# Order on VectorE's queue at the end of a half: the addition of two accumulators, the turning of the next pair, and dispatch steps

## The chip, the cores and the metric

The kernel runs on one core of one Trainium2 chip. The metric is the device time of one execution in microseconds (us). Three timed executions of the kernel before took 711.72, 712.66 and 712.91 us; their median, 712.66 us, is the time that the change is measured against. The profile shows one further execution, of 712.75 us, with a span of 711.0 us from the first to the last instruction of the program.

## The reference

Two stages in a row. The first is attention with a block mask (`_attn_ref`), on 4 batches of 8 heads, 768 positions and a head size of 64, all float32:

```
scores = scale * np.matmul(q, k.transpose(0, 1, 3, 2))
scores = np.where(mask, scores, -1000000000.0)
attn = np.exp(scores - max) / (sum + 1e-09)
x = np.matmul(attn, v)
```

The mask keeps blocks of 32 x 32: the diagonal and its neighbours, the first and last block row and column, and three sampled blocks per block row. The second stage (`_moe_ref`) takes the 3072 rows of 512 numbers, finds for each row the nearest of 8 experts by cosine similarity (largest logit), and passes the row through that expert alone: a matrix product with w1 (512 x 1024), a maximum with 0, a matrix product with w2 (1024 x 512), and a multiplication by the gate, the largest softmax probability.

## The kernel before

**Attention** (`attention_fast`, from L928). The work is cut into 192 units. A unit `u` belongs to a pair of heads (`g`, 12 units each, 16 pairs), to one half of the queries (`qh`, 384 of 768) and to one block of 128 keys (`kc`, 0 to 5). Six units make up a *half*: 384 queries of two heads against all keys. There are 32 halves.

For each unit, `score_fast` (L348) puts the mask and the scores into a PSUM tile `sc` by 12 groups of small matmuls (L358) and lets ScalarE take the exponential into a tile `e` (L361; four buffers, in the pool `ep`). `attend_fast` (L365) multiplies the values with `e` on TensorE and gathers the products of a half in PSUM, in the tile `av` (L379). The pool `acc` that holds `av` has one buffer, of two banks: one sum over the even and one over the odd 64 keys of each block. On VectorE the tiles `e` of a half are added up into `esum`, which gives the denominators later: the first addition of a half is L374 (`kc == 1`), the other four are L376. At the end of a half ScalarE copies one of the two accumulators into `part` (L383), and VectorE adds the other to it, giving `at` (L385). That addition is the last reader of `av`, so the first value matmul of the next half waits for it.

`settle` (L389), three units into the next half, turns `at` and `esum` back on TensorE (L407, L414) and divides on VectorE (L417 to L427). `squares` (L431) then takes the sum of squares of those rows on GpSimd (L438, L442).

**The next pair** is loaded by `load_blocks` (L254, its DMAs in L264, on SyncE's queue SP except for some of the first) and `load_pair` (L250), and turned by `turn_blocks` (L267): VectorE transposes its blocks of 32 x 32, first those of k (`kt<-kld`), and one unit later those of q (`qt<-qld`), two instructions each (L274). The raw tiles `kld` and `qld` have one buffer each, so the load of the pair after next follows the turn.

**Routing and dispatch** (`route` L491, `rank` L550, `dispatch_early` L655) are generators. After every batch, `after_sequence` (L910) makes a plan by hand: at which unit of the next batch which step is taken. The steps of `dispatch_early` come in the units 1, 2 and 4 of a half, from unit 22 on in the third batch and up to unit 8 in the fourth. The last batch is routed in `last_rows` (L1077), amid the first expert tile.

**Expert tiles** (`expert_tile` L835, `mixed_tile` L873). Rows are gathered by expert in tiles of 128, the matrix products run on TensorE, and the weights, 4 MB for each tile, come in by DMA (L807).

**Order.** The framework puts the instructions of each engine into one queue when the program is built. It keeps to the order of the source among what its model takes to be ready, but it may move one instruction ahead of another. `issue_after(x)` forbids that for one case: each instruction made inside the block which runs on the same engine as `x` stands behind `x` in that engine's queue. It adds no semaphore. In `attention_fast` the planned steps stand behind `n.summed`, `n.exps` and `n.tick` (L980: VectorE, ScalarE, SyncE), and `turn_blocks` behind `n.summed` (L988). In the kernel before, `n.summed` is always the newest addition into `esum` (L374 or L376), never `at`.

Of the kernel before, what the change touches and what calls it, by code (L numbers as in the profile page):

```python
# [15 lines left out]
ALU = mybir.AluOpType  # L16
# [8 lines left out]
NC = S // P  # L25
# [21 lines left out]
HALF = S // 2  # L47
# [317 lines left out]
def attend_fast(k, u):  # L365
    nc = k.nc
    g, qh, kc = u // (2 * NC), u // NC % 2, u % NC
    e, v = k.es[u], k.loaded[g][2]
    if kc == 0:
        k.av = k.acc.tile([P, 2, 512], F32, name="av", tag="av")  # L370
        k.first = e
    elif kc == 1:
        k.esum = k.sp.tile([P, 2, HALF], F32, name="esum", tag="esum")
        k.summed = nc.vector.tensor_tensor(out=k.esum, in0=k.first, in1=e, op=ALU.add)  # L374
    else:
        k.summed = nc.vector.tensor_tensor(out=k.esum, in0=k.esum, in1=e, op=ALU.add)  # L376
    for r in range(2):
        for h in range(2):
            nc.tensor.matmul(k.av[D * h:D * (h + 1), r, 0:HALF], lhsT=v[D * r:D * (r + 1), h, kc, :],  # L379
                             rhs=e[D * r:D * (r + 1), h, :], start=(kc == 0), stop=(kc == NC - 1))  # L380
    if kc == NC - 1:
        part = k.sp.tile([P, HALF], F32, name="part", tag="part")
        nc.scalar.copy(out=part, in_=k.av[:, 1, 0:HALF])  # L383
        at = k.sp.tile([P, HALF], F32, name="at", tag="at")
        nc.vector.tensor_tensor(out=at, in0=k.av[:, 0, 0:HALF], in1=part, op=ALU.add)  # L385
        k.done[u // NC] = (at, k.esum)


# [85 lines left out]
def logits(k, x):  # L474
    nc, p = k.nc, k.rp
    lg = two_banks(k, "lg")[:, 0, 0:NC * E].rearrange("p (c e) -> p c e", e=E)
    for c2 in range(0, NC, 2):
        ps = k.big.tile([P, 2 * ND, P], F32, name="xt_ps", tag="big")
        for i in range(2 * ND):
            c, d = c2 + i // ND, i % ND  # L480
            nc.tensor.transpose(ps[:, i, :], x[:, c, d * P:(d + 1) * P], k.ident)
        xt = p.tile([P, 2 * ND, P], F32, name="xt")
        nc.vector.tensor_copy(out=xt, in_=ps)
        for c in (c2, c2 + 1):
            for d in range(ND):
                nc.tensor.matmul(lg[:, c, :], lhsT=xt[:, (c - c2) * ND + d, :], rhs=k.en[:, d, :],
                                 start=(d == 0), stop=(d == ND - 1))
    return lg


def route(k, b):  # L491

    nc, p, x = k.nc, k.rp, k.x[b]
    nrm = p.tile([P, NC], F32, name="nrm")
    if k.exact:
        for c in range(NC):
            sq = p.tile([P, DM], F32, name="sq")
            nc.scalar.activation(sq, x[:, c, 0:DM], ACT.Square, accum_out=nrm[:, c:c + 1])
    else:
        nsq = k.nsq[b]  # L500
        nc.gpsimd.tensor_tensor(out=nsq[:, :, 0:2], in0=nsq[:, :, 0:2], in1=nsq[:, :, 2:4], op=ALU.add)
        nc.gpsimd.tensor_tensor(out=nrm.unsqueeze(2), in0=nsq[:, :, 0:1], in1=nsq[:, :, 1:2], op=ALU.add)
    nc.gpsimd.tensor_tensor(out=nrm, in0=nrm, in1=k.half, op=ALU.pow)

    def wide(t):
        return t.unsqueeze(2).broadcast_to([P, NC, E])

    l = p.tile([P, NC, E], F32, name="l")
    lg = logits(k, x) if k.exact else l
    if not k.exact:  # L510
        part = k.part[b]
        for w in (4, 2):
            nc.gpsimd.tensor_tensor(out=part[:, :, 0:w], in0=part[:, :, 0:w], in1=part[:, :, w:2 * w], op=ALU.add)
        nc.gpsimd.tensor_tensor(out=l, in0=part[:, :, 0], in1=part[:, :, 1], op=ALU.add)
    yield
    nc.vector.tensor_scalar(out=nrm, in0=nrm, scalar1=1e-6, scalar2=None, op0=ALU.add)
    nc.vector.reciprocal(out=nrm, in_=nrm)
    m = p.tile([P, NC], F32, name="mx")
    nc.vector.tensor_tensor(out=l, in0=lg, in1=wide(nrm), op=ALU.mult)
    nc.vector.reduce_max(out=m, in_=l, axis=AX.X)  # L520
    nc.vector.tensor_tensor(out=l, in0=l, in1=wide(m), op=ALU.subtract)
    yield
    ex = p.tile([P, NC, E], F32, name="ex_l")
    nc.scalar.activation(ex, l, ACT.Exp)
    oh = k.oh[:, b * NC:(b + 1) * NC, :]
    pick = p.tile([P, NC, E], F32, name="pick")
    nc.vector.tensor_scalar(out=pick, in0=l, scalar1=0.0, scalar2=None, op0=ALU.is_equal)
    nc.vector.tensor_tensor(out=pick, in0=pick, in1=k.rev.unsqueeze(1).broadcast_to([P, NC, E]), op=ALU.mult)
    nc.vector.reduce_max(out=m, in_=pick, axis=AX.X)
    nc.vector.tensor_tensor(out=oh, in0=pick, in1=wide(m), op=ALU.is_equal)  # L530
    yield
    for c in range(NC):
        t = b * NC + c
        nc.gpsimd.tensor_tensor(out=k.seen[:, t + 1, :], in0=k.seen[:, t, :], in1=k.oh[:, t, :], op=ALU.add)
    for w in (4, 2):
        nc.gpsimd.tensor_tensor(out=ex[:, :, 0:w], in0=ex[:, :, 0:w], in1=ex[:, :, w:2 * w], op=ALU.add)
    gate = x[:, :, DM:XW]
    nc.gpsimd.tensor_tensor(out=gate, in0=ex[:, :, 0:1], in1=ex[:, :, 1:2], op=ALU.add)
    nc.gpsimd.tensor_scalar(out=gate, in0=gate, scalar1=1e-9, scalar2=None, op0=ALU.add)
    yield  # L540
    nc.vector.reciprocal(out=gate, in_=gate)
    yield
    drams = (k.x_early, k.x_dram) if b < EARLY else (k.x_dram,)
    for dram in drams:
        for c in range(NC):
            nc.sync.dma_start(out=dram[b * S:(b + 1) * S, :].rearrange("(c p) w -> p c w", c=NC)[:, c], in_=x[:, c])
            yield
# [362 lines left out]
def after_sequence(n, b):  # L910

    routing = partial(next, route(n, b), None)
    plan = [(7, routing), (14, routing), (16, routing), (17, routing), (20, partial(rank, n, b)), (23, routing)]
    plan += [(27 + NC * (i // 4), routing) for i in range(NC * (1 + (b < EARLY)))]
    if b == EARLY - 1:
        n.dispatching = partial(next, dispatch_early(n), None)
        plan += [(u, n.dispatching) for u in range(22, 45) if u % NC in (1, 2, 4)]
    if b == EARLY:
        plan += [(u, n.dispatching) for u in (1, 2, 4, 8)]
        plan += [(9, partial(fetch_rows, n, 0)), (10, partial(fetch_rows, n, 1))]  # L920
        for i, when in enumerate(((3, 3, 3, 9, 9, 9, 15, 15), (15, 21, 21, 21, 33, 33, 39, 39))):
            step = partial(next, fetch_weights(n, i, i, 4), None)
            plan += [(u, step) for u in when]
        plan += [(44, partial(prepare, n, 0))]
    return plan


def attention_fast(n, ctx):  # L928
# [34 lines left out]
    for u in range(units):  # L963
# [14 lines left out]
        for when, what in plan:  # L978
            if when == u % (per * NPAIR):
                with n.tc.issue_after(n.summed.ins), n.tc.issue_after(n.exps.ins), n.tc.issue_after(n.tick.ins):  # L980
                    what()

        steps = [partial(attend_fast, n, u)] + ([partial(score_fast, n, u + 2)] if u + 2 < units else [])
        for step in reversed(steps) if u % NC == 0 else steps:
            step()
# [12 lines left out]
def attention_exact(n, ctx):  # L998
# [14 lines left out]
    for u in range(units + 2):  # L1013
        if u < units:
            if u % per == 0 and u // per + 2 < pairs:
                load_pair(n, u // per + 2)
            score(n, u)
            if u % per == per - 3 and u // per + 1 < pairs:
                turn_pair(n, u // per + 1)
        if 1 <= u <= units:  # L1020
            turn_probs(n, u - 1)
        if u >= 2:
            attend(n, u - 2)
            if (u - 1) % (H * NC) == 0:
                b = (u - 1) // (H * NC) - 1
                for _ in route(n, b):
                    pass
                rank(n, b)
                if b == EARLY - 1:
                    for _ in dispatch_early(n):  # L1030
                        pass
# [145 lines left out]
```

## Time and profile before

| | |
|---|---|
| median of three runs | 712.66 us |
| profiled execution, its span | 712.75 us, 711.0 us |
| busy, share of the span: TensorE | 98% |
| VectorE, ScalarE, GpSimd | 47%, 27%, 32% |
| `sc` matmuls, q and k (L358) | 1536, 157.9 us |
| `av` matmuls (L379) | 1536, 154.9 us |
| `hp` matmuls of the experts (L845) | 1472, 169.1 us |
| `yp` matmuls (L858) | 368, 162.0 us |
| additions into `esum` (L374, L376) | 160, 162.3 us |
| additions `at` (L385) | 32, 0.55 us each |

How it is read: a row of the page's groups has the line, the engine, the operation, what it writes and reads, and the count; then busy us and ns of one; then the idle time of the engine just before these instructions, and who ended most of it. A row of the timeline has the start in us, the us that it covers, and the instruction; square brackets hold the idle time before it and its releaser. A row of the windows has the stretch, its length, and for each engine its busy us with the number of instructions.

Attention fills roughly the first 331 us; the expert tiles take the rest. PE is TensorE's matmuls, PEld its weight loads, DVE VectorE, ACT ScalarE, POOL GpSimd, SP SyncE.

### The profile page before, as it was taken

The page shows a single profiled execution, that of the slowest core. Times are in us where ns is not written, and L with a number is a line of the kernel's source. Part 1 is how long each engine was busy: PE and PEld are TensorE (multiplying, and loading weights), DVE is VectorE, ACT ScalarE, POOL GpSimd, SP SyncE. Part 2 cuts the span into 40 slices and gives each one's busy share as a digit, 9 for nine tenths or more (in the row PEclk, how much of TensorE's full clock was granted, in tenths as well). Part 3 has the DMA queues.
Part 4 walks back from the last instruction along what each step waited for, and adds up shares of the span by engine and source line. Part 5 has one row for each costly group of instructions (what it writes and reads, how often), then busy time and mean ns, then how long its engine had stood idle before and what let it go on. Part 6 is the DMA issues. An engine that isn't in the chain of part 4 may idle for free.

```text
span 711.0 us, 19426 instructions
## 1 busy us (share of the span) xinstructions
PE 693.6 (98%) x8313; PEld 436.5 (61%) x8313; DVE 332.6 (47%) x684; ACT 188.5 (27%) x266; POOL 230.0 (32%) x383
## 2 busy tenths in 40 slices
PE   9999999999999999999999999999999999999992
PEld 4555555555555554557767777676676756667771
DVE  6887778777878888765661111111111111111110
ACT  5455545555555455453000000000000000000000
POOL 1255466544764367545401111112111111112010
PEclk9999999999999999999999999999999999999997
DMA  7632333575326768553999989988899998999990
GB/s 133 116 63 43 59 68 69 128 135 122 65 41 155 127 157 219 193 165 113 274 398 397 368 319 344 337 321 302 313 405 397 400 333 313 404 396 396 343 320 18
DMA packets 180808, 164.76 MB, mean 232 GB/s; under 512 B 128284, under 2 KB 128284, under 8 KB 180710
## 3 DMA queue, kind: packets, MB, share of 16 engines
q1 hardware_dynamic: 174950, 149.80, 67.1%
q0 software_dynamic: 4160, 13.39, 4.8%
q8 instruction: 69, 1.13, 0.7%
q10 hardware_dynamic: 1600, 0.20, 0.2%
q14 instruction: 29, 0.24, 0.1%
HBM read 147.62 MB, written 16.01 MB: 230 GB/s over the span
## 4 chain that ended last, share of the span: by engine, by line
PE 90%; issue 3%; DVE 3%; POOL 1%; ACT 1%; DMA 1%; POOLq 0%; DVEq 0%; SPq 0%; ACTq 0%
PE hp L845 21%; PE yp L858 21%; PE sc L358 20%; PE av L379 17%; PE back L414 3%; PE hp L886 2%; PE yp L906 2%; PE xg_ps L830 1%; PE back L407 1%; ACT e L361 1%; PE warm L80 1%; DVE kt L274 1%; DVE esum L376 1%; DVE at L385 0%; DMA out_dram<-y,slot_l 0%
## 5 line engine op out<-in xcount | busy, mean ns | idle before, releaser
L361 ACT ACTIVATE e<-sc 128x768 f32<-128x768 f32 x192 | 155.7, 811 | 154.9 <-PE sc L358 149.7
L845 PEld LDWEIGHTS hp<-xgt,w 128*128 128x128 f32 x1472 | 167.7, 192 | 10.8 <-issue 10.2
L845 PE MATMUL hp<-xgt,w 128*128 128x128 f32 x1472 | 169.1, 275 | 0.0
L858 PE MATMUL yp<-w,h 128*128 128x512 f32 x368 | 162.0, 593 | 0.1
L358 PE MATMUL sc<-qt,kt 64*64 64x384 f32 x1536 | 157.9, 482 | 0.0
L379 PE MATMUL av<-e,vld 64*64 64x384 f32 x1536 | 154.9, 487 | 3.0 <-DVE at L385 2.8
L376 DVE TENSOR_TENSOR esum<-esum,e 128x768 f32<-128x768 f32 x128 | 131.6, 1028 | 40.4 <-ACT e L361 38.6
L858 PEld LDWEIGHTS yp<-w,h 128*128 128x128 f32 x368 | 68.0, 190 | 77.5 <-issue 76.3
L442 POOL TENSOR_TENSOR sq<-sq 128x192 f32<-128x192 f32 (+1 forms) x186 | 106.0, 570 | 13.9
L867 POOL DMA_INDIRECT out_dram<-y,slot_l x20 | 20.2, 1008 | 246.0 <-DVE y L866 233.9
L848 ACT ACTIVATE h<-hp 128x512 f32<-128x512 f32 x23 | 13.7, 597 | 298.3 <-PE hp L845 298.3
L379 PEld LDWEIGHTS av<-e,vld 64*64 64x64 f32 x1536 | 53.8, 133 | 61.0 <-issue 28.2
L866 DVE TENSOR_SCALAR y<-yp,xg 128x512 f32<-128x512 f32 x25 | 18.8, 751 | 140.7 <-PE yp L858 128.2
L358 PEld LDWEIGHTS sc<-qt,kt 64*64 64x64 f32 x1536 | 58.9, 133 | 38.5 <-issue 36.2
L852 DVE TENSOR_SCALAR h<-hp 128x512 f32<-128x512 f32 x23 | 15.9, 692 | 131.6 <-PE hp L845 131.6
L438 POOL TENSOR_TENSOR sq<-x 128x384 f32<-128x384 f32 x31 | 27.1, 874 | 121.9 <-DVE part L427 101.9
L358 PE MATMUL sc<-qmask,kmask 64*64 64x384 bf16 x768 | 65.9, 323 | 0.1
L358 PEld LDWEIGHTS <-kmask 64*64 64x64 bf16 x768 | 24.7, 107 | 33.1 <-issue 33.0
L374 DVE TENSOR_TENSOR esum<-e 128x768 f32<-128x768 f32 x32 | 30.7, 959 | 10.0 <-ACT e L361 9.4
L414 PE MATMUL back<-ones,esum 64*64 64x1 f32 x1536 | 26.4, 190 | 0.0
L414 PEld LDWEIGHTS back<-ones,esum 64*64 64x64 f32 x1536 | 25.6, 135 | 0.0
L785 POOL DMA_INDIRECT xg<-x_dram,slot_l x22 | 22.6, 1027 | 6.7 <-issue 6.7
(191 smaller groups left out, 361.4 us busy)
## 6 DMA issues: line engine op xcount, KB each, us to landing
w<-in_moe_w_dram SPq DMA_DIRECT2D x54, 2048.0 KB
w<-in_moe_w_dram SPq DMA_DIRECT2D x16, 512.0 KB
x_dram<-x SPq DMA_DIRECT2D x24, 256.5 KB
vld<-in_v_dram SPq DMA_DIRECT2D x32, 192.0 KB
kld<-in_k_dram SPq DMA_DIRECT2D x60, 96.0 KB
qld<-in_q_dram SPq DMA_DIRECT2D x60, 96.0 KB
x_early<-x SPq DMA_DIRECT2D x12, 256.5 KB
ticks<-dens SPq DMA_DIRECT2D x32, 0.0 KB
```

The lines of the kernel that those rows point to most:

```text
L358: nc.tensor.matmul(ps[D * r:D * (r + 1), h, 0:HALF], lhsT=rows[D * h:D * (h + 1), keys], rhs=cols[D * h:D * (h + 1), queries], start=first ...
L361: k.exps = nc.scalar.activation(e, ps[:, :, 0:HALF], ACT.Exp, scale=SCALE)
L374: k.summed = nc.vector.tensor_tensor(out=k.esum, in0=k.first, in1=e, op=ALU.add)
L376: k.summed = nc.vector.tensor_tensor(out=k.esum, in0=k.esum, in1=e, op=ALU.add)
L379: nc.tensor.matmul(k.av[D * h:D * (h + 1), r, 0:HALF], lhsT=v[D * r:D * (r + 1), h, kc, :], rhs=e[D * r:D * (r + 1), h, :], start=(kc == 0 ...
L414: nc.tensor.matmul(sums[D * s:D * (s + 1), t, h, r:r + 1], lhsT=esum[D * r:D * (r + 1), h, cols], rhs=k.ones[D * r:D * (r + 1), 0:1], star ...
L438: nc.gpsimd.tensor_tensor(out=sq, in0=x, in1=x, op=ALU.mult)
L442: k.squared = nc.gpsimd.tensor_tensor(out=out, in0=sq[:, :, 0:width], in1=sq[:, :, width:2 * width], op=ALU.add).ins
L785: k.nc.gpsimd.indirect_dma_start(out=x[:, :], out_offset=None, in_=(k.x_dram if late else k.x_early)[:, :], in_offset=bass.IndirectOffsetO ...
L845: nc.tensor.matmul(hp[:, f, :], lhsT=w1[:, d, (f0 + f) * P:(f0 + f + 1) * P], rhs=xt[:, d, :], start=(d == 0), stop=(d == ND - 1))
L858: nc.tensor.matmul(yp, lhsT=h[:, f, :], rhs=w2[:, f, :], start=(f == 0), stop=(f == NF - 1))
L867: nc.gpsimd.indirect_dma_start(out=k.out[:, :], out_offset=bass.IndirectOffsetOnAxis(ap=slot, axis=0), in_=y[:, :], in_offset=None, bounds ...
```

## The change

It adds no instruction of an engine and takes none away. Three things are set differently for the order of VectorE's queue:

1. At the end of a half, `n.summed` becomes the addition `at` instead of staying the last addition into `esum`. So what is put behind `n.summed` in the units 0 and 1 of the next half (turning of the next pair, planned steps), and after unit 5 of the first half, stands behind `at`.
2. The first addition of a half (`kc == 1`, L374) is put behind `n.summed`, thus behind `at` of the half before. For the first half it is put behind the last exponential, an instruction of ScalarE.
3. In `route`, the reciprocal of the gates (L541) is put behind the comparison that picks the expert (L530).

```diff
@@ attend_fast
     elif kc == 1:
         k.esum = k.sp.tile([P, 2, HALF], F32, name="esum", tag="esum")
-        k.summed = nc.vector.tensor_tensor(out=k.esum, in0=k.first, in1=e, op=ALU.add)
+        with k.tc.issue_after(k.summed.ins if u > NC else k.exps.ins):
+            k.summed = nc.vector.tensor_tensor(out=k.esum, in0=k.first, in1=e, op=ALU.add)
...
-        nc.vector.tensor_tensor(out=at, in0=k.av[:, 0, 0:HALF], in1=part, op=ALU.add)
+        k.summed = nc.vector.tensor_tensor(out=at, in0=k.av[:, 0, 0:HALF], in1=part, op=ALU.add)
@@ route
-    nc.vector.tensor_tensor(out=oh, in0=pick, in1=wide(m), op=ALU.is_equal)
+    picked = nc.vector.tensor_tensor(out=oh, in0=pick, in1=wide(m), op=ALU.is_equal).ins
...
-    nc.vector.reciprocal(out=gate, in_=gate)
+    with k.tc.issue_after(picked):
+        nc.vector.reciprocal(out=gate, in_=gate)
```

## The prediction

> **What bounds the kernel now.** I read the page first: busy shares, slices, and the group of the value matmuls (L379).
>
> ```profile
> PE 693.6 (98%) x8313; PEld 436.5 (61%) x8313; DVE 332.6 (47%) x684; ACT 188.5 (27%) x266; POOL 230.0 (32%) x383
> DVE  6887778777878888765661111111111111111110
> L379 PE MATMUL av<-e,vld 64*64 64x384 f32 x1536 | 154.9, 487 | 3.0 <-DVE at L385 2.8
> ```
>
> TensorE is busy 98% of the span, and the chain that ended last lies 90% on PE. The first 18 or so slices are attention, where VectorE too is busy six to eight tenths; after that it nearly idles. Only a gap of PE in attention can be won back. Next the table of waits, for who makes those gaps (columns: us in total, times, longest).
>
> ```profile
> PEld av L379 <- DVE at L385: 17.5, 30, 1.3
> PE av L379 <- DVE at L385: 2.8, 7, 0.7
> ```
>
> The accumulator `av` is a single buffer, so the first value matmul of a half waits until `at` (L385) has read the previous half's sums. The 17.5 us are idle time of the weight loads, which run ahead of the matmuls; only 2.8 us show as gaps of the matmuls. But a matmul's end is modelled, so I count from start to start, in the timeline. An ordinary half boundary, VectorE and then PE:
>
> ```profile
> 58.56 0.56 DVE L385 TENSOR_TENSOR at<-av,part 128x384 f32<-128x384 f32 x1 [0.44 <-ACT part L383]
> ```
> ```profile
> 58.72 0.82 PE L358 MATMUL sc<-qt,kt 64*64 64x384 f32 x8
> 59.36 0.82 PE L379 MATMUL av<-e,vld 64*64 64x384 f32 x8
> ```
>
> From the last score group to the first value group: 0.64 us. `at` started 0.03 us after ScalarE's copy `part` (58.05 to 58.53) and made nobody late. A boundary at which the next pair is turned:
>
> ```profile
> 48.00 1.02 DVE L274 STREAM_TRANSPOSE kt<-kld 128x384 f32<-128x384 f32 x2
> 48.95 0.51 DVE L385 TENSOR_TENSOR at<-av,part 128x384 f32<-128x384 f32 x1
> 49.59 0.96 DVE L374 TENSOR_TENSOR esum<-e 128x768 f32<-128x768 f32 x1
> ```
> ```profile
> 48.66 0.82 PE L358 MATMUL sc<-qt,kt 64*64 64x384 f32 x8
> 49.52 0.88 PE L379 MATMUL av<-e,vld 64*64 64x384 f32 x8
> ```
>
> `part` was there at 48.48, but VectorE was turning kt; `at` came 0.48 us late and PE's step is 0.86: 0.22 lost, and about 0.05 more in the restart (0.88 for 0.82, periods of 9.84 after such a half). A boundary with a dispatch step as well:
>
> ```profile
> 228.57 1.02 DVE L274 STREAM_TRANSPOSE kt<-kld 128x384 f32<-128x384 f32 x2
> 229.53 0.21 DVE L605 TENSOR_TENSOR at_e<-oh,taken 128x96 f32<-128x96 f32 x1
> 229.77 0.25 DVE L608 TENSOR_REDUCE taken_t<-at_e 128x12 f32<-128x96 f32 x1
> 229.94 0.55 DVE L385 TENSOR_TENSOR at<-av,part 128x384 f32<-128x384 f32 x1
> ```
> ```profile
> 229.24 0.82 PE L358 MATMUL sc<-qt,kt 64*64 64x384 f32 x8
> 230.54 0.88 PE L379 MATMUL av<-e,vld 64*64 64x384 f32 x8 [0.48 <-DVE at L385]
> ```
>
> The step is 1.30: 0.66 lost.
>
> **What the Trainium skill says.** "PSUM — Partial Sum Buffer", Engine vs sequencer instructions: VectorE's queue is strict FIFO. The trace agrees: `at` stood behind two transposes with its operands ready for 0.48 us. "Perfetto Trace Analysis", Optimization Strategy: a gap repeating on the engine that should be saturated can mean too few buffers. It agrees: the gap recurs every second half, at the one accumulator. "SBUF — State Buffer", Who interferes with whom: a VectorE instruction with two SBUF inputs contends with a GpSimd one that reads SBUF. It agrees: L376 takes 0.96 alone and 1.33 beside the squares (L438, L442). The change adds no such overlap.
>
> **The change part by part.** Nothing is added or removed; instructions change places in VectorE's queue.
>
> (a) *`at` ahead of kt's turn and of the dispatch steps of units 0 and 1 of a half.* I take, for each of the 31 boundaries, the start-to-start step beyond 0.64. First half: 0.85 (two transposes and two copies L237 stand before `at`). Halves that only turn a pair: 0.21, 0.21, 0.21, 0.38, 0.08, 0.22, 0, 0.37, 0.08, sum 1.76. Halves with dispatch steps, av restarting at 210, 220, 231, 241 and 251 us: 0.22, 0.16, 0.66, 0.42, 0.63, sum 2.09. The half at 272 us: 0.77. Together 5.47; with some 15 restarts of 0.05, **6.2 us**. It all lies on the path, since PE is the chain there, and all goes if `at` starts when `part` ends: `at` takes 0.56, so at 48.48 it would end at 49.06, and PE wants it at about 49.30. At 272 us the sum before it ends at 270.75, `at` then at 271.3, PE wants 271.5: gone as well.
>
> (b) *What waits behind `at` now.* VectorE stands still from the end of the last sum to the end of `part`, at most the copy's 0.47 us, where it turned kt before. So kt moves about 1.0 us later (0.48 + 0.51), the first sum of the half (L374), qt and the second sum about 0.5. Who waits: the exponential of unit 4 needs the buffer that L374 frees; L374 ends at 50.5 now, 51.0 then, and that exponential starts at 53.4, so 2.4 us hide it. The third sum waited 0.42 us for ScalarE, which absorbs most of the rest. Price nothing in plain halves. The turned tiles are read by the next pair, some 17 us later.
>
> (c) *The turn's DMAs.* Each kt and qt turn frees the buffers of eight loads (L264) on SP's queue: kld from 49.05, qld until 54.9. They go 0.5 to 1.0 us later, and with them the vld, ticks, x and weight issues queued behind. The next turn starts at 67.8, and kt waited for its load only twice, 1.8 us, both at the start: over 10 us hide it. Price nothing.
>
> (d) *Full VectorE.* In the dispatch stretch its slack is small (window, us, then PE, PEld, DVE busy):
>
> ```profile
> 229.00:239.50 10.50, 10.02 (x196) 5.41 (x192) 9.49 (x24) 5.23 (x8) 4.14 (x9) 1.00 0.97 153
> 249.80:260.30 10.50, 10.05 (x196) 5.41 (x192) 9.42 (x18) 5.21 (x8) 4.50 (x9) 1.00 0.72 137
> ```
>
> A half without stalls is 9.79 on PE. 9.49 + 0.47 is 0.17 more than that, 9.42 + 0.47 is 0.10 more, and each is followed by a half with about 2 us free. Cost between 0 (the next half takes it) and 0.5; I take 0.2.
>
> (e) *The first sum queued behind `at`.* In the trace L374 follows `at` at every boundary: it moves only as in (b). For unit 1 the edge names an instruction of ScalarE and orders nothing on VectorE.
>
> (f) *Gates' reciprocal behind the pick.* In three batches it already is (125.6 behind 114.2, 205.6 behind 194.3, 288.6 behind 277.3). In the last it comes first:
>
> ```profile
> 344.13 0.19 DVE L541 RECIPROCAL x<-x 128x6 f32<-128x6 f32 x1 [0.73 <-POOL x L539]
> 344.81 0.19 DVE L529 TENSOR_REDUCE mx<-pick 128x6 f32<-128x48 f32 x1
> 345.03 0.21 DVE L530 TENSOR_TENSOR oh<-pick,mx 128x48 f32<-128x48 f32 x1
> ```
>
> L529 and L530 fit into the 0.73 us of waiting, so `oh` comes 1.2 us earlier, and POOL's six `seen` additions (345.32, 1.61 us) can end near 345.7. PE's rank matmuls read `seen` at 347.03, just behind; gain at most 0.1. The loss: if POOL takes `seen` ahead of the gate sums, the reciprocal slips 1.6 us, xgt (L832) may stand behind it until about 347.5, and PE starts tile 1 up to 0.8 later. I take 0.
>
> Sum: −6.2 + 0.2 + 0 = **−6.0 us** on the span of 711.0, so 705.0. The expert stage has no PE wait for weights in the table of waits; it starts earlier by the same amount. The profiled execution took 712.75, the three timed ones 711.72 to 712.91: the span is 1.7 below, and the difference carries over. 712.66 − 6.0 = **706.7**.
>
> **Rivals.** *Half the gain*: the dispatch steps pushed behind `at` find VectorE full, and the boundaries from 210 to 272 us stay late by another wait (2.86 us of the 5.47 and six restarts of 0.05, so 3.1 of the 6.2 are kept): 712.7 − 3.1 = 709.6. For it: 9.49 of 10.5 busy. Against: that 10.5 itself contains the stall, and the half between is at 7.92. *Nothing moves*: the queue keeps its order, or some other ready instruction slips ahead of `at`: 712.7. Against: kt, dispatch and the first sum are the only ones that stand there. *Slower*: VectorE becomes the bound because it holds still for `part`. At 15 turns of 0.47 us, 7.1 us come back as late sums, buffers freed late, and exponentials that hold up scores: 712.7 − 6.0 + 7.1 = 713.8, more with gaps elsewhere. It decides once a half's VectorE work plus 0.47 exceeds 9.79, that is 9.3 of work; the other turning halves have some 8 to 8.8 in such windows, and only these two of 15 are above.
>
> **How the numbers follow.** Forecast 0.79, half the gain 0.12, nothing moves 0.04, slower 0.05. The forecast's own range is 705.7 (the full 6.2, the reciprocal's 0.1, and 0.6 for the spread of the runs) to 708.3 (0.5 in (d), 0.8 in (f), 0.3 elsewhere). Stretched toward the second case: 705.7 to 709.4. A difference of 0.2% (1.4 us) is about what measurement can tell from none. Faster: 0.79 + 0.12 = 0.91; same 0.04; slower 0.05.
>
> **What would show it.** Right: `at` starts about 0.03 us after `part` at every boundary, kt behind it; the wait of PE's av for `at` falls from 2.8 to under 0.3; periods of 9.8 in attention; the last exponential near 322.4 instead of 328.4. In the last batch L530 ahead of L541. Wrong: new waits of ACT e for DVE esum, dispatch halves still above 10.2, or a hole of PE before tile 1.

## The result, and the profile after

The changed kernel took 706.30 us (median of 6, 706.12 to 706.84) against 712.46 us (median of 6, 711.62 to 712.92) of the kernel before on the same chip: a ratio of 0.9916, with a 95% interval of 0.9903 to 0.9929. That is 6.2 us less by the medians (the interval says 5.1 to 6.9); 6.0 were forecast. The profiled execution took 706.15 us, its span went from 711.0 to 704.4 us. In the changed kernel most lines of attention stand one lower (`at` is L386, `av` L380, `part` L384, the sums L375 and L377), those of routing one or two, those of the experts two.

The page, its busy shares and the group of the value matmuls:

```profile
PE 690.1 (98%) x8313; PEld 445.2 (63%) x8313; DVE 332.4 (47%) x684; ACT 188.4 (27%) x266; POOL 229.0 (33%) x383
L380 PE MATMUL av<-e,vld 64*64 64x384 f32 x1536 | 155.8, 486 | 0.0
```

No count of instructions has changed, and PE's share is 98% as before: the page's first part would not show that anything happened. The last column does: the idle time ahead of `av` is 0.0, where it was 3.0. The window from the first to the last half boundary, where PE's busy time stands first after the length:

```profile
18.20:316.00 297.80, 297.80 (x5802) 174.92 (x5799) 239.58 (x466) 157.60 (x214) 161.59 (x282) 1.00 0.52 114
```

PE has no gap at all in 297.8 us; before, the like stretch (19.39 to 322.30 us) had 300.61 busy of 302.91. The table of waits (total, times, longest, in us), the third row from the kernel before:

```profile
DVE at L386 <- ACT part L384: 13.8, 30, 0.8
PEld av L380 <- DVE at L386: 9.2, 30, 0.5
```
```profile
DVE at L385 <- ACT part L383: 8.2, 15, 0.9
```

The row of PE's matmuls waiting for `at` is gone. The weight loads wait half as long as before (17.5), and the wait that comes instead is VectorE's own, for ScalarE's copy: 13.8 us, up from 8.2. That is the price in (b) of the prediction, and TensorE does not pay it. A boundary at which the next pair is turned, VectorE and then PE in the timeline:

```profile
47.32 0.56 DVE L386 TENSOR_TENSOR at<-av,part 128x384 f32<-128x384 f32 x1 [0.43 <-ACT part L384]
47.79 1.03 DVE L274 STREAM_TRANSPOSE kt<-kld 128x384 f32<-128x384 f32 x2
48.74 0.91 DVE L375 TENSOR_TENSOR esum<-e 128x768 f32<-128x768 f32 x1
```
```profile
47.47 0.83 PE L358 MATMUL sc<-qt,kt 64*64 64x384 f32 x8
48.12 0.83 PE L380 MATMUL av<-e,vld 64*64 64x384 f32 x8
```

`at` starts 0.03 us after `part` (46.81 to 47.29), kt stands behind it, and PE's step is 0.65. The dispatch boundary with the two short steps, which was 1.30 before:

```profile
225.48 0.56 DVE L386 TENSOR_TENSOR at<-av,part 128x384 f32<-128x384 f32 x1 [0.43 <-ACT part L384]
225.96 1.03 DVE L274 STREAM_TRANSPOSE kt<-kld 128x384 f32<-128x384 f32 x2
226.91 0.22 DVE L607 TENSOR_TENSOR at_e<-oh,taken 128x96 f32<-128x96 f32 x1
227.16 0.25 DVE L610 TENSOR_REDUCE taken_t<-at_e 128x12 f32<-128x96 f32 x1
```
```profile
225.64 0.82 PE L358 MATMUL sc<-qt,kt 64*64 64x384 f32 x8
226.28 1.15 PE L380 MATMUL av<-e,vld 64*64 64x384 f32 x12
```

The step is 0.64. I call the time from the end of `part` to the start of `at` the *lag*, and the time from the first value matmul of a half to the first of the next half the *period*. In the changed kernel the lag is 0.03 at 30 of 31 boundaries (0.14 at one). The period is 9.79 but for the first half (8.71), the last (9.76), the five halves that hold more matmuls on PE (10.3 to 10.8 here, up to 11.1 before) and one of 9.84.

Summed by period, before against after: first half 1.19 (0.28 of it because the first value matmul of all came that much earlier in this execution), halves that only turn a pair 1.73, dispatch halves 2.19, the half at 272 us 0.77, ten restarts of 0.05. That is 6.38, and the first value matmul of the last half starts at 315.91 instead of 322.30: 6.39. Counted from the first value matmul of all it is 306.39 instead of 312.50 us, 6.11 less; I call this the *attention stretch*. From the last half on both kernels take the same steps; PE's first product of expert tile 1 starts 6.43 earlier, its last matmul ends 6.44 earlier. The routing of the last batch in between, on VectorE:

```profile
336.17 0.68 DVE L854 TENSOR_SCALAR h<-hp 128x512 f32<-128x512 f32 x1
336.76 0.20 DVE L529 TENSOR_TENSOR pick<-pick,rev 128x48 f32<-128x48 f32 x1
336.88 0.68 DVE L834 COPY xgt<-xg_ps 128x512 f32<-128x512 f32 x1
337.48 0.19 DVE L530 TENSOR_REDUCE mx<-pick 128x6 f32<-128x48 f32 x1
337.71 0.21 DVE L531 TENSOR_TENSOR oh<-pick,mx 128x48 f32<-128x48 f32 x1
337.83 0.19 DVE L543 RECIPROCAL x<-x 128x6 f32<-128x6 f32 x1
```

The pick (L530, L531) is ahead of the reciprocal, as the third edit says. GpSimd's additions `seen` start at 338.00; `oh` was at 345.03 before and is 7.32 earlier, of which 6.43 is the general shift. PE reads `seen` at 340.60, 1.0 us after its end; no wait of PE for it shows in either kernel.

### The profile page after: what moved, and what is told of

Its sections match the earlier page's. It is cut to its first block, busy times and chain, and to the rows that moved or that the text cites. A ratio compares the mean times of both kernels' runs of the same rounds, so it can differ in the third digit from the quotient of the medians.

```text
span 704.4 us, 19430 instructions
## 1 busy us (share of the span) xinstructions
PE 690.1 (98%) x8313; PEld 445.2 (63%) x8313; DVE 332.4 (47%) x684; ACT 188.4 (27%) x266; POOL 229.0 (33%) x383
## 4 chain that ended last, share of the span: by engine, by line
PE 94%; issue 2%; POOL 1%; DVE 1%; DMA 0%; ACT 0%; POOLq 0%; DVEq 0%; ACTq 0%
PE sc L358 22%; PE hp L847 21%; PE yp L860 21%; PE av L380 18%; PE back L415 3%; PE hp L888 2%; PE yp L908 2%; PE back L408 2%; PE xg_ps L832 1%; PE warm L80 1%; DMA out_dram<-y,slot_l 0%; POOL xg L787 0%; PE hp L900 0%; POOL sq L443 0%; ACT e L361 0%
## 5 line engine op out<-in xcount | busy, mean ns | idle before, releaser
L847 PEld LDWEIGHTS hp<-xgt,w 128*128 128x128 f32 x1472 | 167.7, 192 | 10.8 <-issue 10.2
L358 PE MATMUL sc<-qt,kt 64*64 64x384 f32 x1536 | 159.7, 482 | 0.0
L380 PE MATMUL av<-e,vld 64*64 64x384 f32 x1536 | 155.8, 486 | 0.0
L377 DVE TENSOR_TENSOR esum<-esum,e 128x768 f32<-128x768 f32 x128 | 129.7, 1013 | 32.6 <-ACT e L361 29.2
L443 POOL TENSOR_TENSOR sq<-sq 128x192 f32<-128x192 f32 (+1 forms) x186 | 101.1, 544 | 13.9
L380 PEld LDWEIGHTS av<-e,vld 64*64 64x64 f32 x1536 | 57.9, 133 | 50.9 <-issue 23.1
L358 PEld LDWEIGHTS sc<-qt,kt 64*64 64x64 f32 x1536 | 61.2, 133 | 36.3 <-issue 32.1
L854 DVE TENSOR_SCALAR h<-hp 128x512 f32<-128x512 f32 x23 | 15.9, 691 | 131.5 <-PE hp L847 131.5
L358 PE MATMUL sc<-qmask,kmask 64*64 64x384 bf16 x768 | 67.9, 323 | 0.1
L439 POOL TENSOR_TENSOR sq<-x 128x384 f32<-128x384 f32 x31 | 29.2, 941 | 117.1 <-DVE part L428 99.7
L358 PEld LDWEIGHTS <-kmask 64*64 64x64 bf16 x768 | 26.6, 107 | 31.0 <-issue 29.3
L375 DVE TENSOR_TENSOR esum<-e 128x768 f32<-128x768 f32 x32 | 31.4, 982 | 8.0 <-ACT e L361 8.0
```

The costliest lines, as they stand in the source:

```text
L358: nc.tensor.matmul(ps[D * r:D * (r + 1), h, 0:HALF], lhsT=rows[D * h:D * (h + 1), keys], rhs=cols[D * h:D * (h + 1), queries], start=first ...
L439: nc.gpsimd.tensor_tensor(out=sq, in0=x, in1=x, op=ALU.mult)
L443: k.squared = nc.gpsimd.tensor_tensor(out=out, in0=sq[:, :, 0:width], in1=sq[:, :, width:2 * width], op=ALU.add).ins
L847: nc.tensor.matmul(hp[:, f, :], lhsT=w1[:, d, (f0 + f) * P:(f0 + f + 1) * P], rhs=xt[:, d, :], start=(d == 0), stop=(d == ND - 1))
```

## The experiments

The kernels a1 to a4 and b1 are edits of the kernel before, the others of the changed one.

**a1: the new meaning of `n.summed` alone.** Only `k.summed` becomes `at` (the second edit in the order of the diff); the first sum and the reciprocal are left as before.

```diff
-        nc.vector.tensor_tensor(out=at, in0=k.av[:, 0, 0:HALF], in1=part, op=ALU.add)
+        k.summed = nc.vector.tensor_tensor(out=at, in0=k.av[:, 0, 0:HALF], in1=part, op=ALU.add)
```

> Only the second edit: the addition of the two accumulators becomes the newest addition, the first sum and the reciprocal are queued as in the kernel before. Theory (the whole gain is the addition's place ahead of the turns and dispatch steps): as the changed kernel, 706.3 us. Rival (the edge on the first sum or the reciprocal carries part of it): above 707.

Measured 706.87 us (5 runs) against 712.59, ratio 0.9915 (0.9902 to 0.9929). VectorE's queue is that of the changed kernel except for the reciprocal's place, and the attention stretch is 306.42 us, the changed kernel's 306.39. So the whole gain comes from this one line, and the edge on the first sum changes nothing.

**a2: the reciprocal alone.** The third edit, as in the diff of the change.

> Only the third edit: the gates' reciprocal behind the pick. Theory: 712.5, no change within 0.1, because the rank matmuls that need the pick come no earlier than the expert products before them on TensorE; in the trace GpSimd's six additions into seen start about 1.2 us earlier relative to the pick's first step. Rival (the pick held up the first tile): 711.7 or less, and TensorE reaches the second tile sooner.

Measured 712.33 us (13 runs), ratio 0.9996 (0.9988 to 1.0004): nothing, as expected. Its attention stretch is 312.04 us, the kernel before's 312.50: by so much do two traces differ whose order in attention is the same.

**a3: only the turning behind `at`.** The planned steps stay ahead of it.

```diff
+        k.ended = nc.vector.tensor_tensor(out=at, ...)
...
-            with n.tc.issue_after(n.summed.ins):
+            with n.tc.issue_after(n.summed.ins), n.tc.issue_after(n.ended.ins):
                 turn_blocks(n, g + 1, turn)
```

> Only the turning of the next pair goes behind the addition; planned steps stay ahead of it. From the terms of the forecast: 0.65 of the first half's 0.85, the plain turning halves in full (1.76), 0.22 + 0.66 + 0.63 of the dispatch halves that also turn, 0.77 at 272 us, and 13 restarts of 0.05: 5.3 us, so 707.2 and at most 0.4 lower. The two halves with dispatch steps alone keep their 0.16 and 0.42. Rival (the parts add up by the count of instructions moved, half of them dispatch): about 709.5.

**a4: only the planned steps behind `at`.** The same `k.ended`, named at the planned steps; the turning stays ahead.

```diff
-                with n.tc.issue_after(n.summed.ins), n.tc.issue_after(n.exps.ins), ...:
+                with n.tc.issue_after(n.summed.ins), n.tc.issue_after(n.exps.ins), ..., \
+                        n.tc.issue_after(n.ended.ins):
                     what()
```

> Only the planned steps go behind the addition; the turns stay ahead of it. From the terms: 0.16 + 0.42 of the halves with dispatch alone, 0.44 + 0.41 where a turn stays ahead and leaves its 0.22, two restarts: 1.5 us, so 711.0. With the run that moves the turns alone this makes 6.8, more than the 6.2 of both, since either one heals most of the two shared halves. Rival (strict addition): 712.5 less what the other run leaves of 6.2, so 711.6.

a3 took 708.33 us, ratio 0.9942 (0.9929 to 0.9956): 4.3 us gained, 5.3 expected. a4 took 711.15 us, ratio 0.9979 (0.9969 to 0.9989): 1.4 gained, 1.5 expected. In a3 all the plain turning halves are at 9.79 with a lag of 0.03, so that part is confirmed. The trace's attention stretch is 1.32 us longer than the changed kernel's; 1.14 of that lies at the dispatch boundaries, where 0.58 and two restarts had been left standing. (The whole span is 2.2 us longer; the other 0.9 lies in the start, ahead of tile 1 and in the close of the program, which vary by such amounts among the twelve traces.) VectorE and PE at one of the dispatch boundaries in a3 (the kernel before's line numbers):

```profile
225.30 0.64 DVE L605 TENSOR_TENSOR at_e<-oh,taken 128x96 f32<-128x96 f32 x1
225.97 0.25 DVE L608 TENSOR_REDUCE taken_t<-at_e 128x12 f32<-128x96 f32 x1
226.14 0.55 DVE L385 TENSOR_TENSOR at<-av,part 128x384 f32<-128x384 f32 x1
```
```profile
225.96 0.82 PE L358 MATMUL sc<-qt,kt 64*64 64x384 f32 x8
226.74 1.52 PE L379 MATMUL av<-e,vld 64*64 64x384 f32 x16
```

L605 took 0.21 in the kernel before, where it stood behind the turning, and takes 0.64 here; the step of PE is 0.78 for 0.64. I had priced the two short steps from the row of before. Why L605 is longer in the new place was not tried. The traces give a lead: 0.53 of the 0.64 us lie beside one of GpSimd's additions of squares (L442); in b1 it took 0.88, of which 0.76 beside L438; where it took 0.21 to 0.27, at most 0.19 lay beside them. In a4 the converse is seen, at a plain turning boundary:

```profile
48.44 1.03 DVE L274 STREAM_TRANSPOSE kt<-kld 128x384 f32<-128x384 f32 x2
49.39 0.52 DVE L385 TENSOR_TENSOR at<-av,part 128x384 f32<-128x384 f32 x1
```

The lag is 0.48 and the period 10.00, exactly as before. The two parts give 4.3 and 1.4 by the medians, together 5.7 of 6.2. The attention stretches give 4.8 and 2.1, together 6.9 for 6.1, as the expectation of a4 had it; neither the medians, with intervals 1.9 and 1.4 us wide, nor single traces, which differ by 0.5 in a2, decide it. At the boundary with both kinds of work shown above, PE's step was 0.66 too long before, and is 0.14 too long in a3 and 0.21 in a4: either kind alone is enough to be late, and moving either alone heals most.

**b1: another cure.** If the loss comes from what stands ahead of `at`, turning two units later, in the middle of the half, should cure it without any edge.

```diff
-        turn = u % per - (0 if g else NC - 1)
+        turn = u % per - 2
```

> The kernel before with the turning put into the units 2 and 3 of a half in place of 0 and 1, and no edge to the addition at all. Theory (what costs is a turn standing ahead of the addition): the same 5.3 us as with the turns queued behind it, 707.2. Rival (the edge itself, or the new place of the loads on SP's queue, makes the gain): 712.5 or, with the loads later still, above.

Measured 713.52 us (12 runs), ratio 1.0012 (1.0003 to 1.0021): 0.9 us slower, where 707.2 was expected. The first boundary did not change: in VectorE's queue kt still stands ahead of `at` there, with a lag of 1.08, though the source names later units. The plain turning halves are at 9.79 with a lag of 0.03, so the turning was the cause there. But the work had to go somewhere. In the halves that route a batch VectorE now runs late at the end of the half:

```profile
116.57 0.95 DVE L376 TENSOR_TENSOR esum<-esum,e 128x768 f32<-128x768 f32 x1
117.43 0.55 DVE L385 TENSOR_TENSOR at<-av,part 128x384 f32<-128x384 f32 x1
```
```profile
118.04 1.52 PE L379 MATMUL av<-e,vld 64*64 64x384 f32 x16 [0.27 <-DVE at L385]
```

Here it is the last sum itself that stands ahead of `at`; the lag is 0.67, the period 10.24. The like happens at 198 and 281 us (10.23, 10.46), at 239 us behind dispatch steps (10.98), and the half that ends at 271 us takes 11.56 with no lag at all: PE's scores come late inside it, for a cause I did not find. The attention stretch is 311.67 us, so that 0.8 us are left of a gain of 6.1. And 2.0 us are lost behind the last matmul: the program's close takes 14.98 us there, 12.8 to 13.2 in the other eleven traces. GpSimd's waits at L1143, the end of the check of rows, are 2 us later; why is open.

**d1 and d2: a measured delay put ahead of `at`.** One or two spare transpositions of `esum`, of the size of kt's, stand ahead of `at` at 15 of the boundaries that do not turn. They add work and leave nothing out.

```diff
+        if (u // NC) % 2 == 0 and u >= 2 * NC:
+            spare = k.sp.tile([P, HALF], F32, name="spare", tag="spare", bufs=1)
+            for _ in range(1):  # d2: range(2)
+                with k.tc.issue_after(k.summed.ins):
+                    k.summed = nc.vector.transpose(out=spare..., in_=k.esum[:, 0]...)
+        with k.tc.issue_after(k.summed.ins):
+            k.summed = nc.vector.tensor_tensor(out=at, ...)
```

> The changed kernel, with one spare transposition of 128 x 384 put ahead of the addition in the 15 boundaries that turn nothing. It starts when the last sum ends, 0.40 us before the copy ends, and lasts 0.5: the addition is some 0.05 to 0.15 late, under the 0.27 that TensorE leaves. Theory (a delay counts only beyond 0.27): 706.3, no change. Rival (every delay of the addition is paid): 0.1 a boundary, 707.8, or the full 0.5 of the instruction, 713.8.

> The same with two spare transpositions, as long as a turn of k: the addition 0.48 late, 0.21 lost and 0.05 for the restart at 14 boundaries (the last one has more room): 3.7 us, so 710.0, and periods of 10.0 and 9.84 at the boundaries again. Rival (it was the turn's loads or buffers, not the time on VectorE): 706.3.

d1 took 708.87 us, ratio 0.9941 (0.9925 to 0.9958), 2.6 more than the changed kernel where nothing was expected. d2 took 716.01 us, ratio 1.0043 (1.0026 to 1.0059), 9.7 more where 3.7 were. (Such differences to the changed kernel, here and below, set medians of different runs of the kernel before side by side, 712.34 to 712.65 us; by the attention stretches they are 2.1 and 10.0, in b2 and b3 3.7 and 10.0.) The boundary at 59 us in d1, then in d2:

```profile
57.38 0.58 DVE L390 STREAM_TRANSPOSE spare<-esum 128x384 f32<-128x384 f32 x1
57.88 0.52 DVE L393 TENSOR_TENSOR at<-av,part 128x384 f32<-128x384 f32 x1
```
```profile
57.82 1.19 DVE L390 STREAM_TRANSPOSE spare<-esum 128x384 f32<-128x384 f32 x2
58.93 0.52 DVE L393 TENSOR_TENSOR at<-av,part 128x384 f32<-128x384 f32 x1
```
```profile
58.36 0.82 PE L358 MATMUL sc<-qt,kt 64*64 64x384 f32 x8
59.50 1.20 PE L380 MATMUL av<-e,vld 64*64 64x384 f32 x12 [0.32 <-DVE at L393]
```

The lags are 0.13 and 0.76, the periods 9.79 and 10.28. The boundaries of d1 and d2, with those of the kernel before and of a4, give one curve of what a lag costs:

| lag, us | 0.03 to 0.22 | 0.34 to 0.35 | 0.39 to 0.40 | 0.48 | 0.75 to 0.76 | 1.00 to 1.01 |
|---|---|---|---|---|---|---|
| lost in the period | 0 | 0.06 to 0.10 | 0.14 to 0.19 | 0.21 | 0.49 to 0.56 | 0.75 to 0.80 |

It is about the lag less 0.26 (0.20 to 0.27), plus the 0.05 of the restart in the half after. The edit moves no turning and no load, so time on VectorE ahead of `at` is enough to cost TensorE what the turning did. The slack can be read in the changed kernel's boundary above: `at` ends at 47.88 and `av` starts at 48.12, 0.24 later, where a late `av` starts 0.05 after `at`; with the lag of 0.03 and the 0.04 by which a late `at` is shorter (0.52 for 0.56) that makes 0.26. Both misses are in the main misses of my lags, not of the curve. In d2 the first spare transposition starts 0.36 us before `part` ends, where kt started 0.48 before it in the kernel before, and the second follows at 0.61 (57.82 and 58.43), where I had counted 0.49: it starts 0.03 after the first has ended, kt's second before its first has ended. At five boundaries of d1 VectorE came late to the single spare one, so that the lag was 0.34 to 0.76; this makes 1.2 of its 2.1 us. But two losses in each have no lag and are outside the curve: the halves that end at 168 and 248 us in d1 (10.14, 10.26; together 0.8), at 172 and 254 us in d2 (10.30, 10.32; the half after 172 too, with 10.47 at a lag of 0.75, lost more than the curve says).

**b2 and b3: more work behind `at`.** To test the rival that VectorE becomes the bound: k is turned twice (I had counted 1.03 us more for VectorE in each turning half), then k and q (2.05 us). The result of the second turning is that of the first.

```diff
+        for _ in range(2 if part is None and n == 0 else 1):  # b3: both n
-        k.turns = k.nc.vector.transpose(...).ins
+            k.turns = k.nc.vector.transpose(...).ins
```

> The changed kernel, with k turned twice, behind the addition: 1.03 us more of VectorE work in each turning half (9.0 to 10.5 us of work there). Theory of the forecast's slower rival (a half must hold its work and the 0.47 of waiting in 9.79): 0 to 0.7 a half, some 4 us, 710. Theory of room (four buffers of e let VectorE lag, and the next half with its 2 us free takes it up): 706.3 to 706.8.

> The changed kernel, with k and q turned twice, behind the addition: 2.05 us more of VectorE work in each turning half, 10.0 to 11.5 us of work there, more than the 9.79 of a half on TensorE. If a half must hold its own work: 0.7 to 2 us at each of 15, some 15 us, 721. If the next half takes it up: 706.3 to 709, the loss in the dispatch halves from 205 to 260 us, where no half is free.

b2 took 710.23 us, ratio 0.9962 (0.9948 to 0.9977): 3.9 more than the changed kernel, some 4 expected by the theory that a half must hold its own work. b3 took 716.41 us, ratio 1.0059 (1.0042 to 1.0076): 10.1 more, between the two expectations. In b2 the plain turning halves stay at 9.79, with the lag 0.03. The losses are in the routing halves at 118, 198 and 280 us (10.40, 10.31, 10.32; together 1.7), where the last sum is late as in b1, in two dispatch halves (0.55), and, with no lag, in three others (1.4): the one that ends at 29 us (10.91 for 10.31, PE waits 0.37 for a copy of the setup, L239), the one at 168 us (late scores) and the one at 249 us (10.13). So the expected 4 us were hit in part by luck. In b3 the plain turning halves are at 9.90 to 9.97 (lag 0.34 to 0.41), two routing halves at 11.25 (lag 1.63) and the third at 11.28 (lag 0.54). So work behind `at` is free up to a point and then comes back, for the most part as the very lag that the change removed.

**b4: the last gap ahead of tile 1.** In the changed kernel `h` of the first expert tile (L854 above, at 336.17) stands in VectorE's queue behind steps of the last batch's routing. b4 puts it and the copy `xgt` ahead of that chain.

```diff
-                meanwhile()
+                next(meanwhile)
...
-            nc.vector.tensor_scalar(out=h[:, half:NF], in0=hp, ...)
+            relu = nc.vector.tensor_scalar(out=h[:, half:NF], in0=hp, ...)
...
+    if meanwhile:
+        with k.tc.issue_after(relu.ins):
+            for _ in meanwhile:
+                pass
```

> The changed kernel, with the maximum of the first tile's second half (and the copy of the next tile's rows) put ahead of the last batch's routing on VectorE, where it waits behind GpSimd's powers. TensorE's gap inside the first tile's second product (7.40 us for 6.87) should close: 0.5 us, 705.8, if the rank matmuls behind it don't wait for seen instead. Rival (they do): 706.3.

PE's products with w2 of that tile, in the changed kernel and in b4:

```profile
333.20 7.40 PE L860 MATMUL yp<-w,h 128*128 128x512 f32 x16
```
```profile
333.69 7.03 PE L864 MATMUL yp<-w,h 128*128 128x512 f32 x16
```

They take 0.37 less (7.03 is also what a later tile takes), and nobody waits for the later `oh`. From the last half's first value matmul to tile 1 b4 takes 24.74 us, the changed kernel 25.12, the other ten traces 25.1 to 25.5. In the times it cannot be told: 706.11 us (705.49 to 706.70), ratio 0.9909 (0.9892 to 0.9925). The first half's `part` ends between 16.7 and 18.1 us in these traces (17.41 in the changed kernel's, 17.99 in b4's), so such a gain is below what the start alone varies by.

## Why the prediction was right

**(a)** carried it, and by its own terms: 1.73 us for the plain turning halves (1.76 forecast), 0.77 for the half at 272 us (0.77), 0.87 for the first half without its earlier start and its restart (0.85; the step of 1.52 in the trace gives 0.88), and 1.99 for the dispatch halves (2.09), once the four restarts inside the 2.19 are taken out. Restarts came to fifteen, as forecast, and to 0.73 us (0.75): ten in halves of their own, four in the dispatch halves, 0.03 in the first. The 0.10 that the dispatch halves fall short is in the one that ends at 207 us, 10.81 in this trace and 10.72 in those of a1, a3 and b4. The step that mattered was to count from start to start: the wait of PE shown in the table of waits was only 2.8 of the 6.4 us, because the ends of matmuls are modelled. a1 shows that this edit alone does it, a3 and a4 that both kinds of work stood in the way, d2 that time alone, put ahead of `at`, costs the like.

**(b)** held for TensorE: VectorE waits 5.6 us longer for `part`, and no new wait of PE shows. ScalarE has two new ones for VectorE, each ahead of an exponential (0.58 us at 234, 0.64 at 270, the first for L428, the second for a sum L377, which was named as a sign of being wrong); both halves keep their 9.79. **(c)** held: PE shows no gap in the whole of attention, so no load came late enough to stop it. **(d)** was priced at 0.2 and cost nothing that shows: the dispatch halves that begin at 207 to 246 us are at 9.79, one at 9.84. Its range began at 0, the right end. Its measure, 9.49 and 9.42 of VectorE's work, came from windows of 10.5 us; from one `at` to the next the same halves have 9.15 and 9.35 in the changed kernel. **(e)** held, by a1. **(f)** held, by a2; the pick came 0.9 us earlier against its surroundings (1.2 forecast), and the loss that was feared did not come, since the reciprocal ran at 337.83, ahead of `seen`. The sum landed closer than the runs can tell, for their interval is 1.8 us wide. One slip in the range changed nothing: its upper end, 708.3, counts 0.2 of (d) twice, and its terms give 708.1.

Of the rivals, *half the gain* fell at the dispatch boundaries of the changed kernel, where no other wait took over. *Nothing moves* fell on the queue itself. *Slower* is a real mechanism, but its point, 9.3 us of work in a half, was too low. From one `at` to the next, VectorE has 8.43 to 8.76 us of work in the plain turning halves of the changed kernel, 9.36 in two routing halves and 9.65 in the third: three routing halves and one dispatch half stand above the point and lose nothing. In b2 a plain turning half has 8.95 and loses nothing; in b3 it has 9.78 and loses 0.18 and a restart, b2's routing halves have 10.2 and lose 0.5 to 0.6. (The doubled turning adds less than its own length: in b2 the last sum starts just ahead of GpSimd's squares and takes 0.95 us, and the first of the squares takes 1.52; in the changed kernel the squares start first and take 0.83, the sum 1.34.) So the point lies near 9.7 in these traces; part of the difference is the slack of 0.26 by which VectorE may be late before TensorE waits, and which the rival had left out. The halves that suffer most are not only those of the dispatch stretch, but the routing halves too, whose last sum comes late.

## What to carry to other kernels

At a buffer that has only one copy, look at what stands ahead of its last reader in that reader's in-order queue, and count the loss from start to start on the bounding engine, not from the rows of idle time. A reader may be late by the slack that the bounding engine has left (0.20 to 0.27 us here) and costs its lateness less that slack beyond. Moving the work away is only as good as its new place: behind the reader it was free, in the middle of the half (b1) it delayed the next reader, and 0.8 of the 6.1 us were left.

## What the runs showed that I had not expected

- The same short VectorE instruction (L605) took 0.21 us behind the turning and 0.64 us when it stood ahead, and two transpositions of `esum` started 0.61 us apart where those of kt start 0.49 apart. The slow L605 ran beside GpSimd's squares, which had started before it (0.53 us of it), and the second of the spare pair started just after the first had ended. No run was made to test either as the cause.
- Halves can lose 0.3 to 0.6 us with no lag of `at` (29, 168 and 249 us in b2, 168 and 248 us in d1, 270 and 280 us in a4). In the one at 168 us in b2 the trace shows score and value matmuls of PE started by ones and threes among each other instead of in groups of eight, and ScalarE waiting 2.51 us for scores. What sets it off is open, and with it some part of each difference between kernels that the lag does not explain.
- The close of the program took 2 us more in b1 than in any other trace (14.98 for 12.8 to 13.2 us after the last matmul), though nothing in that stage was edited.
